# New durations in the cost model that orders a fused attention, FFN and soft-MoE kernel

## The chip, the cores and the metric

The kernel runs on one core of one Trainium2 chip. The metric is the device time of one execution in microseconds (us). The engines are PE (TensorE), DVE (VectorE), ACT (ScalarE), POOL (GpSimd) and SP (SyncE). Each works through its own list of instructions strictly in the order in which the program holds them; an instruction whose inputs are not there holds up everything behind it on its engine.

## The reference

Three stages follow each other, all in float32:

```python
# 1. thresholded attention: q, k, v are (4, 8, 576, 64)
scores = matmul(q, k.T) / 8
thresh = max(scores, -1) - tau
attn = softmax(where(scores >= thresh, scores, -1e9))
x = matmul(attn, v)                     # as (2304, 512)
# 2. FFN: w_in (512, 2048), w_out (2048, 512)
x = relu(x @ w_in)**2 @ w_out
# 3. soft MoE over 2304 tokens, 32 slots, 8 experts
logits = x @ phi
slot_input = softmax(logits, 0).T @ x
slot_out = relu(slot_input[e] @ w1[e]) @ w2[e]   # for each expert e
out = softmax(logits, 1) @ slot_out
```

The weights w_in and w_out reach the chip as 64-bit numbers and are turned into float32 there.

## The kernel before

**The parts of the work.** The conversion takes the two FFN weight matrices in 32 chunks of 128x512: a load on SP (L273), scaling on ACT (`c_scale`, L279), two bit steps on DVE (`c_low` L289, `c_shift` L293), the sign on POOL or DVE (`c_flip` L302, `c_sign` L304). A chunk of w_in is then split into a high and a low part (`c_hi` L319 on ACT, `c_lo` L320 on POOL). A chunk of w_out is turned on PE, multiplied with phi and stored to DRAM (`c_store`, L341).

Attention runs over 16 pairs of heads of five tiles each, 80 tiles in all; the last tile of a pair is mixed and half as large. One tile goes through a chain: the scores on PE (`s`, L477 and L482, or L471 and L474 for a mixed tile), and then for each of its two heads `top` on DVE (L498), `expo` on ACT (L510), `bound` on POOL (L504) and `keep` on DVE (L514). There is one PSUM buffer for the scores, so the scores of the next tile wait for both `top` of this one. From the second batch on, 36 tiles are turned by DMA: `high` on ACT (L532), `low` on POOL (L536), and a DMA transpose on SP (`dturn`, L543); two such tiles make a group, and the group ends with `av` on PE (`av_split`, L635 and L640), which needs both transposes. There are 18 such groups. The other tiles are turned on PE (L241). `hl` (the input of a transpose) has two buffers, `pt` (its output) two.

The FFN has nine units of 256 tokens. A unit is 16 halves of 12 matmuls (`f_a`, `f_b`, L932), followed by relu and square on ACT or DVE, and by a chain of smaller steps towards the slots (L747 to L870). The first half waits for all 32 converted chunks. When attention has ended, the expert weights are loaded, and after the last unit a tail that is written out by hand (`tail`, up to L1176) computes the experts and the output.

**What sets the order.** All of this except the tail is given to a list planner (`Plan`, L31 to L133). Each step has an engine, a modelled duration, a key, the steps it depends on and the buffers it takes and gives back. The planner simulates the engines: whenever one is free it starts, among the steps that are ready by the model and have their buffers, the one with the smallest key. FFN steps have keys on PE above all others (`FKEY`, 1e5), so PE takes them when no attention or conversion step is ready. The modelled durations therefore decide the order of the instructions and nothing else: a semaphore still guards each dependency on the chip. A step that follows another is ready 0.17 (`HOP`) after it. A DMA is modelled as `DMA_LEAD` 1.13, its time on a shared bus, and `DMA_TAIL` 0.95; a transpose also holds SP until its bus time less the tail:

```python
self.bus = max(self.bus, self.now + DMA_LEAD) + o.dma
o.end = max(self.bus, o.end + DMA_LEAD) + DMA_TAIL
if o.turn:
    self.free[o.eng] = max(self.now + o.cost, self.bus - DMA_TAIL)
```

Of the kernel before, what the change touches and what calls it, by code (L numbers as in the profile page):

```python
# [139 lines left out]
def tile_kernel(  # L140
# [26 lines left out]
    NU = 256  # L167
# [45 lines left out]
    def add(kind, eng, cost, fn, deps=(), key=0.0, *args, **kw):  # L213
        return plan.add(eng, cost, fn, deps, key + LEAD.get(kind, 0.0), *args, **kw)
# [41 lines left out]
    def conv_ops():  # L256
# [10 lines left out]
        def chunk(n, w, r0, c0):  # L267
# [72 lines left out]
            g = add("c_turn", "PE", 0.6, turn, [s], k, ["mm", "wt"])  # L340
# [3 lines left out]
            pr = add("c_prod", "PE", 1.05, prod, [e, lphi], k, rel=[("wt", g)])  # L344
# [8 lines left out]
    def attn_ops():  # L353
# [56 lines left out]
        def split_v(x):  # L410
# [39 lines left out]
            sc = add("v_scale", "DVE", 0.5, scales, [st], k0, rel=[("mm", st)])  # L450
# [4 lines left out]
        def tiles(p):  # L455
# [5 lines left out]
            def tile_ops(n, j):  # L461
# [23 lines left out]
                S_ = add("s", "PE", 1.4, s_mm, d["ready"], k, ["s"])  # L485
# [3 lines left out]
                for a in heads:  # L489
# [28 lines left out]
                    X = add("top", "DVE", 0.89, top, [S_], k, ["u"] + (["sm"] if first_g and not a else []), [("s", S_)])  # L518
                    if first_g and not a:
                        gd["first"] = X  # L520
                    h = add("bound", "POOL", 0.52, bound, [X], k)
                    E_ = add("expo", "ACT", 0.77, expo, [X] + ([ee] if a else []), k, [] if a else ["e"])
# [22 lines left out]
                if by_dma(p, g) and not mixed:  # L545
                    ls = []
                    for a in heads:
                        k = key(p, n * TA + a * TA / 2)
                        h = add("high", "ACT", 0.68, lambda a=a: high(a), [ks[a]] + ([hl] if a else []), k, [] if a else ["hl"])
                        hl = hl if a else h  # L550
                        ls.append(add("low", "POOL", 1.72, lambda a=a: low(a), [h], k, rel=[("e", ee)]))
                    k = key(p, n * TA + TA / 2)
                    t = add("dturn", "SP", 3.0, dturn, ls, k, [] if "pto" in gd else ["pt"], [("hl", hl)], dma=-6.8)
# [28 lines left out]
                for x in heads + (2,):  # L582
                    k = key(p, n * TA + min(x, 1) * TA / 2)
                    dep = ks if x == 2 else [ks[x]]
                    new = [] if "pto" in gd else [pk]
                    t = add("turn", "PE", 0.13 if x == 2 else 0.49, lambda x=x: turn(x), dep + [gd.get("pto")], k, ["mm"] + new, [(tag, ee)])
                    v_ = add("p_evac", "ACT", 0.27 if x == 2 else 0.59, lambda x=x: evac(x), [t], k, [], [("mm", t)])
                    gd.setdefault("pto", t)
                    gd.setdefault("turn", []).append(v_)

            def group_ops(g, n):
# [16 lines left out]
                rc = add("recip", "DVE", 0.5, recip, gd["keep"], k, ["rp"], [("sm", gd["first"])])  # L608
# [52 lines left out]
                if g < 2:  # L661
                    rc = add("spread", "POOL", 0.6, spread, [rc], k, ["rb"], [("rp", rc)])
# [13 lines left out]
                rt = add("r_turn", "PE", 0.13 if g == 2 else 0.26, rturn, [rc], k, ["mm", "rr"], rel)  # L676
                rc = add("r_evac", "ACT", 0.3 if g == 2 else 0.4, revac, [rt], k, [], [("mm", rt)])
                deps = gd["turn"] + [d["v_op"], d["vr_op"]]
                first = None
                if by_dma(p, g):  # L680
                    o = first = add("av", "PE", 1.9, av_split, deps + [d["vs_ready"]], k, ["ma"],
                                    [("pt", gd["pto"]), ("vh", d["vs_op"])])
                for lo, hi_ in () if by_dma(p, g) else ((0, 5),) if g == 2 else ((0, 2), (2, 5)):
                    c = (hi_ - lo) * (0.51 if g < 2 else 0.3) 
# [7 lines left out]
                ev = add("evac", "DVE", 0.25 if g == 2 else 0.45, evac, [o, rc], k, ["xp"] if g < 2 and kk == 0 else [], rel)  # L692
# [34 lines left out]
    def ffn_ops(units):  # L727
# [9 lines left out]
        def post(u, d, first, last):  # L737
# [77 lines left out]
            a0 = add("f_pl", "PE", 1.53, lambda: pl(0, MC // NG - 1), d["sq"][:-2], pk(), ["mm"])  # L815
            a = add("f_pm", "PE", 0.51, lambda: pl(MC // NG - 1, MC // NG), [a0] + d["sq"][-2:], pk())
            a2 = add("f_l4", "ACT", 0.26, lambda: nc.scalar.activation(l4, w["pl"][:, :NU], AF.Copy), [a], HI, ["l4"], [("mm", a0)])
            b_ = add("f_p12", "PE", 0.43, p12, [a2], pk(), ["mm"])
            bk = add("f_p1k", "PE", 0.35, p1k, [b_], pk(), [], [("l4", a2)])
            c = add("f_max", "DVE", 0.45, rowmax, [b_, fo.get("nm")], HI)  # L820
            e = add("f_alpha", "ACT", 0.5, alpha, [c, fo.get("nm")], HI, ["dT"], [("mm", b_)])
            f = add("f_total", "DVE", 0.12, total, [e, fo.get("ss")], HI)
            g = add("f_cmax", "DVE", 0.39, cmax, [bk], HI + 1)
            h = add("f_ce", "ACT", 0.15, lambda: nc.scalar.activation(w["ce"], w["ce"], AF.Exp), [g], HI + 1)
            add("f_csum", "DVE", 0.80, csum, [h], HI + 1, rel=[("mm", b_)])
            i_ = add("f_p3", "PE", 0.25, p3, [e], pk(), ["mm"], [("dT", e)])
            j_ = add("f_dk", "DVE", 0.2, dkc, [i_], HI, rel=[("mm", i_)])
            lastsg, turns = fo.get("sg"), []
            for t in range(T):
                gks, ro = [], []  # L830
                for j in range(NG):
# [23 lines left out]
                    ro.append(add("f_gk", "DVE" if dv else "ACT", 0.6 if dv else 0.49, evac, [tt], HI + 2, rel=[("mm", tt)]))  # L855
# [21 lines left out]
                for t_, (accum, merge, ro, gks) in enumerate(turns):  # L877
                    joint = last and t_
                    ac = add("f_acc", "PE", 0.93, accum, ro + [j_] + ([ac0] if joint else []), pk(), [] if joint else ["mm"], gks)
# [8 lines left out]
        for n, u in enumerate(units):  # L888
# [17 lines left out]
            for kk in range(KC):  # L906
# [3 lines left out]
                l = add("xlo", "DVE" if dv else "POOL", 0.35 if dv else 0.69, lambda f=xlo, kk=kk: f(kk), [h] + ls[:1],  # L910
# [5 lines left out]
            for m2 in range(MC // 2):  # L916
# [31 lines left out]
                a = add("f_a", "PE", 1.31, lambda f=mm_half: f(0), hs + ls + ms[-1:] + (conv if n == 0 else []), pk(), ["mm", "gt"])  # L948
                b_ = add("f_b", "PE", 1.31, lambda f=mm_half: f(1), [a], pk())
# [293 lines left out]
```

## Time and profile before

| what | value |
|---|---|
| three runs | 695.98, 696.82, 704.65 us; median 696.82 |
| span of the profiled execution | 694.8 us |
| PE busy | 630.1 us (91% of the span) |
| DVE busy | 456.8 us (66%) |
| ACT busy | 393.2 us (57%) |
| POOL busy | 233.1 us (34%) |
| DMA engines | 104.74 MB, 52% of 16 engines' span |
| mean granted PE clock | 0.979 |

The profile shows one execution. Its own time is not recorded apart from its span, from the first to the last instruction; the median of the three runs is 2.0 us above that span. Busy time counts an instruction until its result is written, so two that follow each other closely overlap a little. Where an engine waited, the row names what ended the wait.

### The profile page before, as it was taken

To read this page: it belongs to the slowest core of one execution; us is meant where nothing else is said; L and a number is where in the kernel's file an instruction comes from. 1 tells how busy PE (TensorE), PEld (TensorE's weight loads), DVE (VectorE), ACT (ScalarE), POOL (GpSimd) and SP (SyncE) were. 2 spreads that over 40 slices of the span, in tenths; PEclk is the share of its full clock that TensorE was granted. 3 is DMA by queue.
4 is the path that set the end of the run, shared out by engine and by line. 5 is a ranking of instruction groups with operands and counts; after the bars stand their busy time and mean duration, and the time that the engine had idled before them with its cause. 6 is when DMAs were issued, how large, how long until landed. Compare 5 with 4: busy or idle time off the path is not lost.

```text
span 694.8 us, 13413 instructions
## 1 busy us (share of the span) xinstructions
PE 630.1 (91%) x5084; PEld 458.4 (66%) x5084; DVE 456.8 (66%) x1183; ACT 393.2 (57%) x762; POOL 233.1 (34%) x308
## 2 busy tenths in 40 slices
PE   1566988999999999999999999999999999998883
PEld 0333656677857686677778667877788989883321
DVE  6999998975787868777966797778733132222503
ACT  4776756766765764766667557757653333331203
POOL 4866433212643434354244344344440000000000
PEclk9987999999999999999999999999999999999998
DMA  6854676422633545163437235352533940397987
GB/s 230 296 180 150 202 246 220 147 93 52 122 70 87 122 70 116 40 135 66 91 73 117 56 69 123 69 122 53 86 59 119 401 174 31 124 371 267 388 321 272
DMA packets 123056, 104.74 MB, mean 151 GB/s; under 512 B 90736, under 2 KB 95856, under 8 KB 122992
## 3 DMA queue, kind: packets, MB, share of 16 engines
q1 hardware_dynamic: 122992, 103.89, 52.0%
q8 instruction: 40, 0.66, 0.4%
q14 instruction: 24, 0.20, 0.1%
HBM read 73.73 MB, written 8.91 MB: 119 GB/s over the span
## 4 chain that ended last, share of the span: by engine, by line
PE 74%; DVE 10%; DMA 5%; ACT 4%; issue 4%; POOL 1%; SPq 0%; DVEq 0%; POOLq 0%; ACTq 0%
PE mm L932 30%; PE mm L241 11%; PE s L482 8%; PE po L627 4%; DVE e L514 3%; PE po L635 3%; PE mm L861 2%; PE mm L747 2%; PE mm L1063 2%; DMA w<-in_moe_w_dram 2%; PE s L477 2%; DMA w_out<-cv 2%; PE s L471 2%; DVE cv L293 2%; ACT e L510 1%
## 5 line engine op out<-in xcount | busy, mean ns | idle before, releaser
L932 PE MATMUL mm<-xh,w 128*128 128x256 f32 x1152 | 167.1, 288 | 0.0
L932 PEld LDWEIGHTS mm<-xh,w 128*128 128x128 f32 x1152 | 147.4, 191 | 16.7 <-issue 10.5
L514 DVE SCALAR_TENSOR_TENSOR e<-u,sm,e 128x576 f32<-128x576 f32 x144 | 125.4, 885 | 26.1 <-ACT e L510 22.9
L498 DVE TENSOR_SCALAR_CACHE_REDUCE u<-s,nscale 128x576 f32<-128x576 f32 x144 | 115.3, 811 | 26.0 <-PE s L482 20.5
L510 ACT ACTIVATE e<-u,sm 128x576 f32<-128x576 f32 x144 | 109.3, 775 | 38.7 <-DVE u L498 36.4
L536 POOL TENSOR_TENSOR hl<-e,hl 128x576 f16<-128x576 f32 x72 | 95.5, 1337 | 84.6 <-ACT hl L532 69.9
L504 POOL TENSOR_SCALAR sm<-sm,tau_p 128x1 f32<-128x1 f32 x144 | 60.7, 424 | 141.1 <-DVE u L498 108.9
L932 PE MATMUL mm<-xl,w 128*128 128x256 f32 x576 | 92.4, 283 | 0.0
L938 ACT ACTIVATE gt<-mm 128x512 f32<-128x512 f32 x72 | 42.9, 596 | 83.3 <-PE mm L932 82.8
L932 PEld LDWEIGHTS mm<-xl,w 128*128 128x128 f32 x576 | 79.3, 192 | 0.0
L482 PE MATMUL s<-kt,qt 64*128 64x512 f32 x256 | 77.0, 680 | 0.0
L241 PE MATMUL mm<-ident_r,e 128*128 128x128 f32 (+1 forms) x332 | 53.3, 296 | 6.0 <-DVE e L514 5.2
L241 PEld LDWEIGHTS mm<-ident_r,e 128*128 128x128 f32 (+1 forms) x332 | 39.9, 151 | 26.8 <-issue 10.0
L477 PE MATMUL s<-kt,qt 128*128 128x128 f32 x128 | 27.2, 295 | 31.0 <-DMA qt<-in_q_dram 11.8
L532 ACT ACTIVATE hl<-e 128x576 f16<-128x576 f32 x72 | 48.1, 679 | 11.8 <-DVE e L514 11.5
L579 ACT ACTIVATE pt<-mm 128x512 f32<-128x512 f32 x72 | 41.7, 594 | 21.9 <-PE mm L241 21.6
L944 DVE SCALAR_TENSOR_TENSOR gt<-mm,gt 128x512 f32<-128x512 f32 x18 | 12.4, 690 | 61.1 <-ACT gt L938 60.3
L477 PEld LDWEIGHTS s<-kt,qt 128*128 128x128 f32 x128 | 20.8, 199 | 36.1 <-issue 19.7
L627 PE MATMUL po<-pt,raw 128*64 128x64 f32 (+1 forms) x480 | 42.0, 309 | 0.0
L241 PE MATMUL mm<-ident_r,gt 128*128 128x128 f32 x288 | 38.3, 278 | 1.4 <-DVE ar L813 1.4
L241 PEld LDWEIGHTS mm<-ident_r,gt 128*128 128x128 f32 x288 | 31.5, 142 | 12.1 <-issue 8.2
L946 ACT ACTIVATE gt<-gt 128x512 f32<-128x512 f32 x54 | 33.9, 627 | 1.1
(148 smaller groups left out, 889.4 us busy)
## 6 DMA issues: line engine op xcount, KB each, us to landing
w<-in_moe_w_dram SPq DMA_DIRECT2D x25, 1024.0 KB, 11.9
raw<-in_moe_w_in_dram SPq DMA_DIRECT2D x16, 512.0 KB, 4.3
raw<-in_moe_w_out_dram SPq DMA_DIRECT2D x16, 512.0 KB, 4.0
kt<-in_k_dram SPq DMA_DIRECT2D x20, 320.0 KB, 3.3
qt<-in_q_dram SPq DMA_DIRECT2D x20, 320.0 KB, 3.7
raw<-in_v_dram SPq DMA_DIRECT2D x20, 256.0 KB, 3.1
w_out<-cv SPq DMA_DIRECT2D x16, 256.0 KB, 4.7
w<-w_out SPq DMA_DIRECT2D x4, 1024.0 KB, 9.1
```

The lines of the kernel that those rows point to most:

```text
L241: nc.tensor.transpose(out_, in_, ident[:n, :n])
L477: nc.tensor.matmul(s[:, 1].rearrange("p (c s) -> p c s", s=64)[:, 0:8:7], lt, d["kt"][:, 512:SQ], start=True, stop=True)
L482: nc.tensor.matmul(s[:, 2 * a], lt[i], d["kt"][i, 0:512], start=True, stop=True)
L498: nc.vector.tensor_scalar(u, o["s"][:, s0:s0 + S], nscale, None, ALU.mult, ALU.min, accum_out=gd["sm"][:, c:c + 1])
L504: nc.gpsimd.tensor_scalar(sm[:, 4 + c:5 + c], sm[:, c:c + 1], tau_p, None, ALU.add)
L510: nc.scalar.activation(e, o["u", a], AF.Exp, scale=-1.0, bias=gd["sm"][:, c:c + 1])
L514: nc.vector.scalar_tensor_tensor(e, o["u", a], sm[:, 4 + c:5 + c], e, ALU.is_le, ALU.mult, accum_out=sm[:, 8 + c:9 + c])
L532: nc.scalar.activation(o["hl"][:, a * S:(a + 1) * S], o["e"][:, a * S:(a + 1) * S], AF.Copy)
L536: nc.gpsimd.tensor_tensor(o["hl"][:, (2 + a) * S:(3 + a) * S], o["e"][:, c], o["hl"][:, c], ALU.subtract)
L627: nc.tensor.matmul(po[i, :n_], lt, rh, start=m == 0, stop=m == 4)
L932: nc.tensor.matmul(o["h"][:, i * NU:(i + 1) * NU], a, c, start=n_ == 0, stop=n_ == len(terms) - 1)
L938: nc.scalar.activation(g, o["h"], AF.Relu)
```

## The change

39 lines with modelled durations get new values; keys, buffers, dependencies and the instructions themselves stay. The core of the diff, with all that concerns attention and the FFN halves:

```diff
-            a = add("c_scale", "ACT", 0.53, scale, [l], k, ["cv"])
+            a = add("c_scale", "ACT", 0.57, scale, [l], k, ["cv"])
...
-                return add("c_lo", "POOL", 1.23, ...
+                return add("c_lo", "POOL", 1.4, ...
...
-                S_ = add("s", "PE", 1.4, s_mm, d["ready"], k, ["s"])
+                S_ = add("s", "PE", 1.28 if mixed else 1.38, s_mm, d["ready"], k, ["s"])
...
-                    X = add("top", "DVE", 0.89, top, ...
+                    X = add("top", "DVE", 0.75, top, ...
...
-                    h = add("bound", "POOL", 0.52, bound, [X], k)
-                    E_ = add("expo", "ACT", 0.77, expo, ...
+                    h = add("bound", "POOL", 0.26, bound, [X], k)
+                    E_ = add("expo", "ACT", 0.67, expo, ...
...
-                    K_ = add("keep", "DVE", 0.92, keep, [E_, h], k, rel=[("u", X)])
+                    K_ = add("keep", "DVE", 0.75, keep, [E_, h], k, rel=[("u", X)])
...
-                        h = add("high", "ACT", 0.68, ...
+                        h = add("high", "ACT", 0.58, ...
...
-                        ls.append(add("low", "POOL", 1.72, ...
+                        ls.append(add("low", "POOL", 1.28, ...
...
-                    t = add("dturn", "SP", 3.0, dturn, ls, k, ..., dma=-6.8)
+                    t = add("dturn", "SP", 2.75, dturn, ls, k, ..., dma=-3.2)
...
-                    o = first = add("av", "PE", 1.9, av_split, ...
+                    o = first = add("av", "PE", 1.83, av_split, ...
...
-                a = add("f_a", "PE", 1.31, ...
-                b_ = add("f_b", "PE", 1.31, ...
+                a = add("f_a", "PE", 1.44, ...
+                b_ = add("f_b", "PE", 1.44, ...
```

**What it moves: PE, the fourth of the 18 groups.** The first four rows are the mixed tile's `av`, and two transposes; then come the scores of a tile and FFN matmuls. Before:

```order
L627 MATMUL po<-pt,raw 64x64 x8
L627 MATMUL po<-pt,vbd_113 64x64 x2
L241 MATMUL mm<-ident_r,rb 128x128 x2
L241 MATMUL mm<-ident_r,rp 128x128
L477 MATMUL s<-kt,qt 128x2x64
L482 MATMUL s<-kt,qt 128x512 x2
L932 MATMUL mm<-xh,w_118 128x256
L932 MATMUL mm<-xh,w_119 128x256
```

Two halves of the FFN (24 matmuls) follow the scores there, then the scores of the next tile, two more halves, and only then the group's `av`. Now, at the same group:

```order
L477 MATMUL s<-kt,qt 128x2x64
L482 MATMUL s<-kt,qt 128x512 x2
L241 MATMUL mm<-ident_r,rb 128x128 x2
L747 MATMUL mm<-gt,wphi 32x256 x16
L241 MATMUL mm<-ident_r,e 128x128 x4
L241 MATMUL mm<-ident_r,e 64x128
L241 MATMUL mm<-ident_r,gt 128x128 x4
L241 MATMUL mm<-ident_r,rp 128x128
L477 MATMUL s<-kt,qt 128x2x64
L482 MATMUL s<-kt,qt 128x512 x2
L635 LDWEIGHTS vh
L635 MATMUL po<-pt,vh 64x256
```

The `av` now stands right behind the scores of the third tile after its group, where four tiles with more FFN work between them stood before.

**SP, the first transposes.** Loads of the next pair (`kt`, `qt`, `raw`) and DMA transposes share this queue. Before:

```order
L543 DMA_TRANSPOSE pt<-hl 128x18x128
L401 DMA kt<-in_k_dram 128x640
L543 DMA_TRANSPOSE pt<-hl 128x18x128
L401 DMA qt<-in_q_dram 128x640
L396 DMA raw<-in_v_dram 128x2x256
L543 DMA_TRANSPOSE pt<-hl 128x18x128 x3
```

Now:

```order
L543 DMA_TRANSPOSE pt<-hl 128x18x128 x2
L401 DMA kt<-in_k_dram 128x640
L401 DMA qt<-in_q_dram 128x640
L396 DMA raw<-in_v_dram 128x2x256
L543 DMA_TRANSPOSE pt<-hl 128x18x128 x3
L401 DMA kt<-in_k_dram 128x640
```

The two loads that stood between and behind the first two transposes now stand behind both.

**DVE, the first attention tile.** Conversion chunks (L289, L293, L304) and attention steps (L498, L514) share DVE at the start. Before:

```order
L293 SCALAR_TENSOR_TENSOR cv<-cv,raw_130 128x512
L304 SCALAR_TENSOR_TENSOR cv<-raw_130,cv 128x512
L289 TENSOR_SCALAR raw_148<-raw_148 128x512
L498 TENSOR_SCALAR u,sm<-s,nscale 128x576
L293 SCALAR_TENSOR_TENSOR cv<-cv,raw_148 128x512
L289 TENSOR_SCALAR raw_156<-raw_156 128x512
L498 TENSOR_SCALAR u,sm<-s,nscale 128x576
L293 SCALAR_TENSOR_TENSOR cv<-cv,raw_156 128x512
L289 TENSOR_SCALAR raw_176<-raw_176 128x512
L304 SCALAR_TENSOR_TENSOR cv<-raw_156,cv 128x512
L293 SCALAR_TENSOR_TENSOR cv<-cv,raw_176 128x512
```

Now:

```order
L293 SCALAR_TENSOR_TENSOR cv<-cv,raw_130 128x512
L304 SCALAR_TENSOR_TENSOR cv<-raw_130,cv 128x512
L498 TENSOR_SCALAR u,sm<-s,nscale 128x576 x2
L289 TENSOR_SCALAR raw_159<-raw_159 128x512
L514 SCALAR_TENSOR_TENSOR e,sm<-u,sm,e 128x576
L293 SCALAR_TENSOR_TENSOR cv<-cv,raw_159 128x512
L289 TENSOR_SCALAR raw_161<-raw_161 128x512
L514 SCALAR_TENSOR_TENSOR e,sm<-u,sm,e 128x576
L293 SCALAR_TENSOR_TENSOR cv<-cv,raw_161 128x512
L289 TENSOR_SCALAR raw_176<-raw_176 128x512
L304 SCALAR_TENSOR_TENSOR cv<-raw_161,cv 128x512
```

The two `top` of the first tile stood two conversion steps apart, the second one six rows below the last step of the fourth chunk; they now follow each other, ahead of the fifth chunk.

## Rows read from the trace of the kernel before

**Rows 1.** Busy time by stage; columns: stretch, length, each engine, granted PE clock, DMA share, GB/s.

```profile
0.00:17.00 17.00, 2.78 (x6) 1.01 (x6) 11.29 (x20) 6.91 (x11) 7.74 (x12) 1.00 0.69 235
17.00:70.00 53.00, 33.56 (x138) 18.35 (x138) 51.62 (x95) 37.71 (x67) 39.18 (x37) 0.86 0.62 208
70.00:122.00 52.00, 46.85 (x329) 32.67 (x330) 46.58 (x118) 35.05 (x68) 20.27 (x25) 0.95 0.70 222
122.00:156.00 34.00, 33.58 (x281) 24.38 (x278) 27.98 (x84) 24.54 (x52) 7.37 (x15) 1.00 0.36 117
156.00:520.00 364.00, 358.35 (x3042) 270.87 (x3042) 269.39 (x738) 237.34 (x468) 153.71 (x213) 1.00 0.43 85
520.00:618.00 98.00, 96.98 (x849) 86.72 (x850) 25.44 (x67) 35.34 (x67) 2.90 (x4) 1.00 0.51 191
618.00:695.00 77.00, 57.96 (x452) 24.37 (x451) 24.51 (x66) 16.33 (x33) 1.90 (x2) 0.94 0.84 317
```

**Rows 2.** Waits of PE, 0 to 156 us: total us, times, longest.

```profile
PE s L477 <- DMA qt<-in_q_dram: 11.8, 1, 11.8
...
PE s L477 <- DVE u L498: 6.6, 1, 6.6
```

**Rows 3.** The chain of waits, 98 to 106 us: start us, us, what.

```profile
99.28 5.93 DMA w_out<-cv
```

**Rows 4.** Groups of instructions, 156 to 520 us: busy us, mean ns, idle before.

```profile
L536 POOL TENSOR_TENSOR hl<-e,hl 128x576 f16<-128x576 f32 x72 | 95.5, 1337 | 84.6 <-ACT hl L532 69.9 <-issue 14.1 <-POOL xl L903 0.2
L514 DVE SCALAR_TENSOR_TENSOR e<-u,sm,e 128x576 f32<-128x576 f32 x106 | 89.1, 856 | 22.1 <-ACT e L510 19.4 <-POOL sm L504 2.2 <-issue 0.4
```

**Rows 5.** The same view, 0 to 156 us.

```profile
L514 DVE SCALAR_TENSOR_TENSOR e<-u,sm,e 128x576 f32<-128x576 f32 x38 | 36.4, 967 | 4.0 <-ACT e L510 3.6 <-ACT cv L279 0.2 <-POOL sm L504 0.2
```

**Rows 6.** Timeline of PE, ACT, SP: the first, seventh, third group; start us, us.

```profile
167.01 1.13 PE L482 MATMUL s<-kt,qt 64*128 64x512 f32 x4
...
176.23 2.67 SPq L543 DMA_TRANSPOSE pt<-hl  x1
...
188.81 1.50 PE L635 MATMUL po<-pt,vh 128*64 128x256 f16 x24
...
287.98 1.13 PE L482 MATMUL s<-kt,qt 64*128 64x512 f32 x4
...
300.57 2.74 SPq L543 DMA_TRANSPOSE pt<-hl  x1
...
190.90 1.13 PE L482 MATMUL s<-kt,qt 64*128 64x512 f32 x4
...
206.29 1.24 ACT L532 ACTIVATE hl<-e 128x576 f16<-128x576 f32 x2
...
210.58 2.67 SPq L543 DMA_TRANSPOSE pt<-hl  x1
```

**Rows 7.** Landing of the transposes, line 543, all 36.

```profile
DMA to landing us min/median/max: 4.5/4.6/6.3
```

**Rows 8.** Pieces of PE work in the chain of waits: start us, us, what.

```profile
155.95 1.44 PE mm L932 x12
159.48 1.06 PE s L482 x4
...
135.39 1.88 PE po L627 x16
...
198.56 1.05 PE s L471 x2
...
213.74 1.46 PE mm L241 x12
...
552.45 2.04 PE mm L747 x32
```

**Rows 9.** The chain of waits in the tail.

```profile
656.10 13.41 DMA w<-in_moe_w_dram
```

More of the change, by code (lines that the diff above doesn't have):

```diff
@@ L308, in chunk @@
             l = add("c_load", "SP", 0.5, load, key=k - 8, acq=["raw64"], dma=1.46)
-            a = add("c_scale", "ACT", 0.53, scale, [l], k, ["cv"])
-            t = add("c_low", on, 0.53 if on == "ACT" else 0.35, low, [l], k)
+            a = add("c_scale", "ACT", 0.57, scale, [l], k, ["cv"])
+            t = add("c_low", on, 0.57 if on == "ACT" else 0.34, low, [l], k)
             s = add("c_shift", "DVE", 0.61, shift, [a, t], k)
             if flip:
-                s = [s, add("c_unit", "ACT", 0.53, unit, [a], k)]
-                s = add("c_flip", "POOL", 1.25, sign, s, k, rel=[("raw64", l)])
+                s = [s, add("c_unit", "ACT", 0.57, unit, [a], k)]
+                s = add("c_flip", "POOL", 1.31, sign, s, k, rel=[("raw64", l)])
             else:
@@ L516, in keep @@
                         )
-                    X = add("top", "DVE", 0.89, top, [S_], k, ["u"] + (["sm"] if first_g and not a else []), [("s", S_)])
+                    X = add("top", "DVE", 0.75, top, [S_], k, ["u"] + (["sm"] if first_g and not a else []), [("s", S_)])
                     if first_g and not a:
                         gd["first"] = X
-                    h = add("bound", "POOL", 0.52, bound, [X], k)
-                    E_ = add("expo", "ACT", 0.77, expo, [X] + ([ee] if a else []), k, [] if a else ["e"])
+                    h = add("bound", "POOL", 0.26, bound, [X], k)
+                    E_ = add("expo", "ACT", 0.67, expo, [X] + ([ee] if a else []), k, [] if a else ["e"])
                     if not a:
                         ee = E_
-                    K_ = add("keep", "DVE", 0.92, keep, [E_, h], k, rel=[("u", X)])
+                    K_ = add("keep", "DVE", 0.75, keep, [E_, h], k, rel=[("u", X)])
                     gd.setdefault("keep", []).append(K_)
@@ L548, in tile_ops @@
                         k = key(p, n * TA + a * TA / 2)
-                        h = add("high", "ACT", 0.68, lambda a=a: high(a), [ks[a]] + ([hl] if a else []), k, [] if a else ["hl"])
+                        h = add("high", "ACT", 0.58, lambda a=a: high(a), [ks[a]] + ([hl] if a else []), k, [] if a else ["hl"])
                         hl = hl if a else h
-                        ls.append(add("low", "POOL", 1.72, lambda a=a: low(a), [h], k, rel=[("e", ee)]))
+                        ls.append(add("low", "POOL", 1.28, lambda a=a: low(a), [h], k, rel=[("e", ee)]))
                     k = key(p, n * TA + TA / 2)
-                    t = add("dturn", "SP", 3.0, dturn, ls, k, [] if "pto" in gd else ["pt"], [("hl", hl)], dma=-6.8)
+                    t = add("dturn", "SP", 2.75, dturn, ls, k, [] if "pto" in gd else ["pt"], [("hl", hl)], dma=-3.2)
                     gd.setdefault("pto", t)
@@ L606, in spread @@
                     nc.gpsimd.tensor_copy(gd["rb"].rearrange("p (t a d) -> p t a d", t=2, a=2), y)
-                rc = add("recip", "DVE", 0.5, recip, gd["keep"], k, ["rp"], [("sm", gd["first"])])
+                rc = add("recip", "DVE", 0.32, recip, gd["keep"], k, ["rp"], [("sm", gd["first"])])
                 def av(lo, hi):
@@ L661, in group_ops @@
                 if g < 2:
[L662 removed]
+                    rc = add("spread", "POOL", 0.38, spread, [rc], k, ["rb"], [("rp", rc)])
                 def rturn():
@@ L691, in group_ops @@
                 rel = [("ma", first), ("rr", rt)] + ([("mx", d["vs_op"])] if by_dma(p, g) else [])
-                ev = add("evac", "DVE", 0.25 if g == 2 else 0.45, evac, [o, rc], k, ["xp"] if g < 2 and kk == 0 else [], rel)
+                ev = add("evac", "DVE", 0.42 if g == 2 else 0.4, evac, [o, rc], k, ["xp"] if g < 2 and kk == 0 else [], rel)
                 ev_at.setdefault("rem" if g == 2 else (b, g), []).append(ev)
@@ L854, in post @@
                     dv = j in GKD
-                    ro.append(add("f_gk", "DVE" if dv else "ACT", 0.6 if dv else 0.49, evac, [tt], HI + 2, rel=[("mm", tt)]))
+                    ro.append(add("f_gk", "DVE" if dv else "ACT", 0.6 if dv else 0.48, evac, [tt], HI + 2, rel=[("mm", tt)]))
                 def accum(t=t):
@@ L909, in ffn_ops @@
                 dv = kk in SPH
-                l = add("xlo", "DVE" if dv else "POOL", 0.35 if dv else 0.69, lambda f=xlo, kk=kk: f(kk), [h] + ls[:1],
+                l = add("xlo", "DVE" if dv else "POOL", 0.34 if dv else 0.71, lambda f=xlo, kk=kk: f(kk), [h] + ls[:1],
                         HI, [] if kk else ["xl"], [] if u == "rem" else [("xp", xdeps[0])])
```

44 lines of the change are left out of this document (22 added, 22 removed).

## Prediction

> **What bounds the kernel now.** I read the engines' busy time by stage first [rows 1]. PE's idle time in the seven stages is 14.2, 19.4, 5.2, 0.4, 5.7, 1.0 and 19.0 us, 64.9 of the 695.0 in all. So there are three regimes. Up to 122 us the conversion of the weights holds PE back: DVE is busy 51.6 of 53.0 us between 17 and 70. From 122 to 618 us PE works 488.9 of 496 us, and the other engines have room (DVE 269.4 of 364.0 while attention and FFN run together). The last 77 us are the hand-written tail. Since all PE work is in the program before and after, the time moves only by what is added to or taken from these 64.9 us: the question is where PE will wait.
>
> In the front PE's longest waits are for the first load, 11.8 us, and for the second `top` of the first tile, 6.6 us [rows 2]; later the chain of waits goes through a store of converted weights, 5.9 us [rows 3]. In the middle I looked at the steps of attention: `keep` takes 856 ns in the mean and `low` 1337 [rows 4]; in the front `keep` takes 967 [rows 5]. Last I followed groups that are turned by DMA, from the end of the scores of their second tile to the issue of the second transpose and to `av` [rows 6], with the time that a transpose needs to land [rows 7].
>
> **The change, part by part.**
>
> *The order.* The planner's DVE and ACT steps become 13 to 18% shorter, `low` 26%; a transpose holds SP for 3.38 instead of 6.98 in the model (1.13 + 3.2 - 0.95 against 1.13 + 6.8 - 0.95). A half of the FFN becomes longer, 1.44 instead of 1.31; the chain of waits has 1.44 for 12 such matmuls [rows 8], so that number is right. The result on PE: before, 55 of the 144 FFN halves stand behind the scores of the last tile, now 76. At 1.44 us, 30 us of FFN work move from between the tiles to behind them. This is no saving: PE does the same work, and where it does nothing but FFN work (520 to 618 us) it is idle 1.0 us [rows 1].
>
> *The front.* The first four chunks and the order of their loads stay. The two `top` of the first tile now follow each other, so the second scores need not wait 6.6 us. But DVE is full there: what attention gains, the conversion loses, and FFN work can start only when all 32 chunks are done. Counted over DVE's list, four more `top` and one more reciprocal pair stand ahead of the last step of the conversion, 4 x 0.86 (the price of `keep`, [rows 4]) and 0.3 (the diff's new value), 3.7 us; PE has one more tile's scores ahead of its first FFN matmul, 1.06 us [rows 8] and two small matmuls. Between 122 and 156 us PE is busy 33.6 of 34.0 us, so the work done earlier there is work not done later. I put the front at 0. If DVE sets the start of the FFN instead, it costs 3.7 us; if the new order of stores and loads removes what PE idles between 70 and 122 us, it gains 5.2.
>
> *The middle, the cover of the transposes.* In the first group 20.7 us passed between the end of the scores (167.01 + 1.13) and `av` (188.81), while the transpose was issued 8.1 us after the scores and landed 4.6 us later, 12.7 us in all [rows 6, 7]. So `av` had 8 us to spare. In the new order I counted the PE work between the same two places, with prices from [rows 8]. In the fourth group: 11 transposes 1.34, two FFN halves 2.88, an `av` of the other kind 1.88 and 0.24, mixed scores 1.05 and 0.24, two scores 2 x 1.30, L747 2.04, 12 transposes 1.46: together 13.7 us. The 18 groups have, in order, 14.0, 15.8, 18.9, 13.7, 14.8, 15.8, 15.1, 23.4, 18.1, 15.9, 17.1, 18.9, 24.1, 55.8, 56.2, 49.0, 19.7 and 18.1 us; before, none had under 19. If all need the 12.7 us of the first, nothing waits: 0. If they need what the seventh needed, 11.5 us to the issue (289.11 to 300.57) and 4.6 to land, 16.1, then seven are short, by 2.1, 0.3, 2.4, 1.3, 0.3, 1.0 and 0.2 us, together 7.6. I take 2: nearer to the lower end, since both the new order of ACT and POOL and the shorter hold of SP work for the short case. On the other side, the most that a better order can take from the stretch 156 to 520 us is its idle 5.7 us; I count none of it.
>
> What queues behind a late `av`: everything on PE, the next scores first, and with them DVE, whose next `top` reads those scores. A stall there is paid in full.
>
> *The port that DVE and POOL share.* Between 0 and 156 us `keep` takes 967 ns against 856 later [rows 4, 5]; the plan now gives it 0.75. The longer means stand beside more POOL work, 74.6 of 156 us against 153.7 of 364.
>
> The Trainium skill ("SBUF — State Buffer", section "Who interferes with whom") says why: a DVE instruction with two SBUF inputs and a GpSimd instruction that reads SBUF exclude each other, and the second one blocks until the first ends. `keep` and `low` are such a pair, and denser attention speaks against the change by that rule. If each group's last `keep` waited out one whole `low` (1.3 us), 12.7 would become 14.0 and the sum would grow by 0.3 us, at the fourth group; the means of the trace show far less than a whole `low` for each.
>
> *The tail.* Its instructions and SP's last rows from the expert weights on are the same. Its longest piece is a load, 13.4 us from 656.1 us on [rows 9]; those loads take the place of tiles that the last FFN unit frees, so they move with the end of the FFN. Cost 0.
>
> *Sum.* 0 + 2 + 0 = +2 us on the span of 694.8. What lies around the span is 2.0 us (the median of the runs, 696.8, less the span), so the forecast is **699 us**, no change that a measurement of this kernel can tell: the bound is 2%, 13.9 us, that is 682.9 and 710.8.
>
> **The rivals.**
>
> *A better order all over (faster).* The new durations of PE, `av` and `low` are nearer to the rows. If PE's waits between 156 and 520 us vanish (5.7) and the idle time between 70 and 122 us with them (5.2), the time is 696.8 - 10.9 = 686. For it: those idle times exist. Against it: the old order already keeps PE at 98.4% there, because its durations for all engines but PE were too long and left cover.
>
> *The cover is gone (slower).* The place is `av` behind the second transpose. Its price starts when scores to landing takes more than 13.7 us, and decides the result above about 17: at 18.0 us eight of the 18 groups are short by 4.0, 2.2, 4.3, 3.2, 2.2, 2.9, 2.1 and 0.9, together 22 us, 697 + 22 = 719. For it: the third group took 18.6 us to the issue alone (192.03 to 210.58). Against it: there `high` was issued only at 206.29 in a line of other work, as the planner had it wait for `hl` buffers that a long modelled transpose kept; that reason falls away.
>
> *The change does nothing.* Excluded: PE's, DVE's, ACT's and POOL's lists all differ, in over a thousand lines on PE.
>
> **Chances and range.** No change around 699 (692 to 706): 0.62. Better all over, 680 to 691: 0.22. Cover gone, 706 to 720: 0.16. Of the second about a quarter lies below 682.9, of the third somewhat over half above 710.8: faster by over 2% 0.05, within 2% 0.86, slower by over 2% 0.09. The range, with 0.1 left out on either side, is 685 to 710.
>
> **What would show each step.** In the new profile, PE's idle time up to its first L932 should be about 39 us, and that matmul start between 152 and 160 us. `av` (L635) should follow the landing of its second transpose by 0 to 6 us instead of 8; PE's waits in front of L635 should sum to 2 us, at most 8. The stretch with attention should end some 30 us earlier, and a longer stretch of nothing but FFN should follow, PE above 98% there, and the tail should take 77 us. The forecast is wrong if PE is idle over 15 us between its first L932 and the end of the FFN, or if the first L932 moves by more than 6 us.

## The result and the profile after

| | before | changed |
|---|---|---|
| median of 20 runs each, us | 698.99 | 707.91 |
| lowest and highest, us | 695.82, 704.65 | 703.75, 711.16 |
| span of the profiled execution, us | 694.8 | 706.7 |
| mean granted PE clock in it, as recorded | 0.979 | 0.969 |

The ratio is 1.0122, with a 95% interval of 1.010 to 1.0143. The changed kernel is slower by 8.9 us in the medians: within the 2% that the forecast called no change, inside its range, and 9 us above its 699.

Busy time by stage of the changed kernel, columns as in [rows 1]:

```profile
0.00:17.00 17.00, 2.77 (x6) 1.00 (x6) 11.24 (x19) 7.47 (x11) 8.97 (x13) 1.00 0.88 277
17.00:70.00 53.00, 33.24 (x139) 18.70 (x141) 52.25 (x96) 34.95 (x66) 36.90 (x36) 0.77 0.57 192
70.00:122.00 52.00, 50.26 (x359) 35.05 (x355) 46.64 (x120) 36.84 (x71) 18.16 (x26) 0.94 0.71 235
122.00:156.00 34.00, 31.36 (x223) 22.33 (x223) 24.36 (x72) 21.83 (x46) 9.32 (x16) 0.95 0.31 100
156.00:520.00 364.00, 350.99 (x2978) 263.87 (x2978) 267.95 (x741) 234.36 (x463) 153.12 (x210) 1.00 0.51 116
520.00:618.00 98.00, 96.96 (x839) 85.82 (x838) 27.22 (x71) 36.05 (x69) 4.37 (x6) 1.00 0.10 34
618.00:707.00 89.00, 68.39 (x551) 35.91 (x549) 25.19 (x67) 20.61 (x40) 1.90 (x2) 0.97 0.86 322
```

PE's idle time rose from 5.7 to 13.0 us in the stretch 156 to 520. The granted clock between 17 and 70 us reads 0.86 before and 0.77 now, but these two do not compare, as the paragraph on the clock below shows. Since attention ends earlier now, stages cut at each kernel's own landmarks compare better: up to the first L932, to the last scores, to the end of the FFN, the tail. The changed kernel:

```profile
0.00:157.90 157.90, 119.53 (x751) 78.68 (x751) 136.31 (x313) 103.00 (x196) 73.35 (x90) 0.89 0.59 193
157.90:474.20 316.30, 303.70 (x2529) 222.17 (x2528) 250.95 (x691) 213.40 (x423) 145.50 (x202) 0.99 0.48 96
474.20:630.50 156.30, 154.85 (x1368) 138.20 (x1370) 43.09 (x115) 59.57 (x114) 12.56 (x15) 1.00 0.36 127
630.50:706.70 76.20, 55.89 (x448) 23.63 (x440) 24.50 (x66) 16.16 (x33) 1.33 (x2) 0.96 0.84 316
```

The kernel before, cut in the same way:

```profile
0.00:155.70 155.70, 116.47 (x745) 76.11 (x746) 137.18 (x313) 103.91 (x195) 74.57 (x89) 0.93 0.60 196
155.70:502.40 346.70, 341.05 (x2877) 256.64 (x2876) 262.82 (x720) 228.94 (x451) 146.30 (x205) 1.00 0.44 87
502.40:618.70 116.30, 115.28 (x1026) 101.73 (x1028) 32.29 (x87) 44.26 (x85) 10.93 (x13) 1.00 0.48 171
618.70:694.80 76.10, 57.26 (x448) 23.89 (x440) 24.51 (x66) 16.11 (x33) 1.29 (x2) 0.94 0.84 316
```

The idle times of PE are 38.4, 12.6, 1.45 and 20.3 us against 39.2, 5.65, 1.0 and 18.8: 72.7 against 64.7 in all, 8.0 us more. PE's busy time for the same work is 634.0 against 630.1 us. The span is 11.9 us longer, and these two are all of it.

**Part of the added busy time is a lower clock.** I took every 5 us of a trace and multiplied PE's busy time there by one minus the granted clock; the sum is the busy time that the lower of the two levels (1.2 instead of 2.4 GHz) added. It is 9.4 us before and 14.5 after. But the records of the clock begin only at 34.2 us in the trace of before and at 21.6 in that of the changed kernel, and up to there the profile states 1.00 for want of a record. The same four matmuls of the scores, in the trace of before, ahead of its first record and behind it:

```profile
30.65 2.08 PE L482 MATMUL s<-kt,qt 64*128 64x512 f32 x4
38.10 1.13 PE L482 MATMUL s<-kt,qt 64*128 64x512 f32 x4
```

All such groups of four ahead of the first record take 2.08 us, in both traces, as does the one at 47.03 us of before, in a stretch recorded at the lower level: PE is at that level there. That adds half of PE's busy time in this stretch (12.2 and 6.4 us), 6.1 us before and 3.2 after. The whole loss to the clock is then 15.5 and 17.7 us, and busy time less this loss is 614.6 and 616.3. So the 11.9 us are 8.0 of waiting, 2.2 of clock and 1.7 that neither accounts for. As far as one profiled execution of each can tell, most of the 8.9 us in the medians is therefore waiting. The same gap in the records lies behind the 0.86 and 0.77 above: with the unrecorded part at the lower level they become 0.70 and 0.73.

**Which waits.** PE's waits between the first L932 and the last scores (total us, times, longest), changed:

```profile
PE mm L241 <- POOL rb L606: 2.5, 2, 1.4
PE mm L241 <- ACT pt L579: 1.4, 1, 1.4
PE mm L747 <- DVE gt L944: 1.1, 1, 1.1
PE s L477 <- DVE u L498: 1.1, 2, 0.8
...
PE po L635 <- DVE u L498: 0.9, 1, 0.9
PE po L635 <- DVE xr L648: 0.9, 1, 0.9
```

The list has fourteen entries, on DVE (4.7 us), ACT (4.3), POOL (2.5) and PE's own queue (0.8). Before, the whole list was four:

```profile
PE mm L861 <- DVE dk L810: 1.8, 2, 1.6
PE s L477 <- DVE u L498: 1.7, 1, 1.7
PE mm L241 <- DVE ar L813: 1.4, 2, 0.7
PE mm L241 <- DVE e L514: 0.7, 1, 0.7
```

No single wait took the place of another; there are many short ones, and ACT and POOL, on which PE never waited here before, now account for over half. One thing that grew is a queue on POOL. The groups of the three steps between 156 and 520 us:

```profile
L514 DVE SCALAR_TENSOR_TENSOR e<-u,sm,e 128x576 f32<-128x576 f32 x107 | 90.5, 859 | 21.9 <-POOL sm L504 12.1 <-ACT e L510 9.0
L536 POOL TENSOR_TENSOR hl<-e,hl 128x576 f16<-128x576 f32 x72 | 94.4, 1328 | 59.2 <-ACT hl L532 55.4 <-issue 2.0 <-POOL sm L504 1.3
L504 POOL TENSOR_SCALAR sm<-sm,tau_p 128x1 f32<-128x1 f32 x104 | 41.8, 406 | 100.1 <-DVE u L498 67.4 <-DVE sm L599 27.2 <-DMA pt<-hl 3.4
```

In [rows 4] DVE waited 2.2 us in front of `keep` for `bound` (`sm`, L504) and 19.4 for `expo`; now it is 12.1 and 9.0. `keep` itself takes 859 ns, as before (856). The new model gives `bound` 0.26, where this row has 406 ns (389 before). `keep` (0.75 in the model, 859 ns in its row) and `low` (1.28 and 1328) are shorter than the trace, too; the old values 0.52, 0.92 and 1.72 stood above it (389, 856 and 1337 before). The chain of waits of the changed kernel shows one such case:

```profile
236.83 0.69 ACT hl L532
237.52 0.07 issue
237.60 2.07 POOL hl L536 x2
239.67 0.44 issue
240.11 0.30 POOL sm L504
240.41 0.02 issue
240.43 0.04 DVE e L514
```

`bound` stands behind two `low` on POOL, which wait for `high`, and `keep` waits for `bound`. The whole piece of the chain off PE runs from 230.56 to 247.03; the pieces of the chain off PE, from the first L932 until attention is done, sum to 83 us, before to 39.

That this queue makes PE wait is not shown. DVE's whole idle time in front of `keep` is no longer than before, 21.9 against 22.1 us, and in the table below e2 has 3.0 us of it on `bound` and still 13.3 us of idle time on PE.

### The profile page after: what moved, and what is told of

Its sections match the earlier page's. It is cut to its first block, busy times and chain, and to the rows that moved or that the text cites. A ratio compares the mean times of both kernels' runs of the same rounds, so it can differ in the third digit from the quotient of the medians.

```text
span 706.7 us, 13443 instructions
## 1 busy us (share of the span) xinstructions
PE 634.0 (90%) x5084; PEld 462.7 (65%) x5084; DVE 454.8 (64%) x1183; ACT 392.1 (55%) x762; POOL 232.7 (33%) x308
## 4 chain that ended last, share of the span: by engine, by line
PE 67%; DVE 13%; DMA 6%; ACT 6%; issue 4%; POOL 1%; SPq 1%; DVEq 0%; ACTq 0%
PE mm L932 28%; PE mm L241 9%; PE s L482 7%; PE po L627 4%; DVE e L514 3%; PE po L635 3%; DVE u L498 3%; PE mm L861 2%; DMA w_out<-cv 2%; PE mm L747 2%; PE mm L1063 2%; DMA w<-in_moe_w_dram 2%; PE s L471 2%; PE s L477 2%; ACT e L510 1%
## 5 line engine op out<-in xcount | busy, mean ns | idle before, releaser
L932 PE MATMUL mm<-xh,w 128*128 128x256 f32 x1152 | 167.0, 287 | 0.4 <-ACT pt L579 0.4
L932 PEld LDWEIGHTS mm<-xh,w 128*128 128x128 f32 x1152 | 147.5, 191 | 17.3 <-issue 14.3
L514 DVE SCALAR_TENSOR_TENSOR e<-u,sm,e 128x576 f32<-128x576 f32 x144 | 125.5, 883 | 29.1 <-ACT e L510 15.6
L498 DVE TENSOR_SCALAR_CACHE_REDUCE u<-s,nscale 128x576 f32<-128x576 f32 x144 | 114.6, 809 | 21.3 <-PE s L482 19.8
L536 POOL TENSOR_TENSOR hl<-e,hl 128x576 f16<-128x576 f32 x72 | 94.4, 1328 | 59.2 <-ACT hl L532 55.4
L504 POOL TENSOR_SCALAR sm<-sm,tau_p 128x1 f32<-128x1 f32 x144 | 58.8, 412 | 133.2 <-DVE u L498 92.8
L932 PE MATMUL mm<-xl,w 128*128 128x256 f32 x576 | 92.4, 283 | 0.0
L932 PEld LDWEIGHTS mm<-xl,w 128*128 128x128 f32 x576 | 79.4, 192 | 0.0
L532 ACT ACTIVATE hl<-e 128x576 f16<-128x576 f32 x72 | 48.1, 682 | 11.9 <-DVE e L514 10.0
L627 PE MATMUL po<-pt,raw 128*64 128x64 f32 (+1 forms) x480 | 44.2, 319 | 0.2 <-ACT pt L579 0.2
L903 POOL TENSOR_TENSOR xl<-xp,xh 128x256 fp32r<-128x256 f32 x16 | 12.1, 768 | 95.3 <-PE mm L932 93.5
## 6 DMA issues: line engine op xcount, KB each, us to landing
w<-in_moe_w_dram SPq DMA_DIRECT2D x25, 1024.0 KB, 11.9
```

The source lines that it names most:

```text
L498: nc.vector.tensor_scalar(u, o["s"][:, s0:s0 + S], nscale, None, ALU.mult, ALU.min, accum_out=gd["sm"][:, c:c + 1])
L504: nc.gpsimd.tensor_scalar(sm[:, 4 + c:5 + c], sm[:, c:c + 1], tau_p, None, ALU.add)
L514: nc.vector.scalar_tensor_tensor(e, o["u", a], sm[:, 4 + c:5 + c], e, ALU.is_le, ALU.mult, accum_out=sm[:, 8 + c:9 + c])
L532: nc.scalar.activation(o["hl"][:, a * S:(a + 1) * S], o["e"][:, a * S:(a + 1) * S], AF.Copy)
L536: nc.gpsimd.tensor_tensor(o["hl"][:, (2 + a) * S:(3 + a) * S], o["e"][:, c], o["hl"][:, c], ALU.subtract)
L627: nc.tensor.matmul(po[i, :n_], lt, rh, start=m == 0, stop=m == 4)
```

## The experiments

They ran in three batches of four; in each the kernel before ran beside them on the same chip (medians 698.5, 699.9 and 699.7 us). Idle times are span less PE's busy time. "Low clock" is the sum over the recorded clock defined above, "start" half of PE's busy time ahead of the first record. The halves are the FFN halves (L932, 12 matmuls) behind the last scores, counted in the trace. The last column is DVE's idle time in front of `keep` put down to `bound`, 156 to 500 us.

| kernel | new on DVE, ACT, POOL | us | ratio (95%) | PE idle | of it first L932 to last scores | low clock | start | halves | `keep` on `bound` |
|---|---|---|---|---|---|---|---|---|---|
| before | no | 699.0 | 1 | 64.7 | 5.6 | 9.4 | 6.1 | 55 | 2.2 |
| e5_vector_back | no | 699.3 | 1.0009 (0.9985-1.0033) | 64.3 | 8.3 | 11.8 | 7.1 | 62 | 3.7 |
| e8_jitter_before2 | no | 704.3 | 1.0084 (1.006-1.0108) | 69.0 | 8.9 | 12.5 | 3.3 | 62 | 0.2 |
| e4_jitter_before | no | 704.7 | 1.0089 (1.0054-1.0125) | 66.3 | 6.6 | 17.4 | 5.7 | 58 | 1.2 |
| e1_pe_only | no | 705.5 | 1.0103 (1.0068-1.0138) | 68.1 | 10.6 | 14.4 | 5.9 | 59 | 1.6 |
| e12_more_slack | no | 706.1 | 1.0079 (1.0051-1.0106) | 64.2 | 6.7 | 16.1 | 8.8 | 60 | 1.9 |
| e3_transpose_only | no | 710.1 | 1.0152 (1.0108-1.0197) | 69.4 | 10.8 | 17.6 | 7.1 | 68 | 3.4 |
| e9_slack | x 1.15 | 709.3 | 1.0116 (1.0086-1.0145) | 65.6 | 10.8 | 18.3 | 6.3 | 75 | 7.7 |
| e11_actpool_back | DVE | 710.1 | 1.0128 (1.0092-1.0165) | 71.9 | 9.6 | 11.6 | 7.6 | 74 | 1.7 |
| e10_dve_back | ACT, POOL | 714.6 | 1.0195 (1.0165-1.0225) | 69.5 | 13.4 | 18.9 | 5.8 | 77 | 15.8 |
| changed | all | 707.9 | 1.0122 (1.010-1.0143) | 72.7 | 12.6 | 14.5 | 3.2 | 76 | 12.1 |
| e7_transpose_back | all | 714.3 | 1.0221 (1.0193-1.0248) | 76.9 | 16.4 | 11.5 | 3.0 | 72 | 6.3 |
| e2_vector_only | all | 718.1 | 1.0278 (1.023-1.0326) | 74.3 | 13.3 | 17.7 | 8.1 | 72 | 3.0 |
| e6_jitter_after | all | 719.1 | 1.0306 (1.0276-1.0336) | 75.9 | 18.5 | 16.2 | 8.3 | 76 | 8.1 |

**First batch: the change in parts, and a meaningless change.** e1 takes the new values of PE alone (14 lines, two shown):

```diff
-                S_ = add("s", "PE", 1.4, s_mm, d["ready"], k, ["s"])
+                S_ = add("s", "PE", 1.28 if mixed else 1.38, s_mm, d["ready"], k, ["s"])
-                a = add("f_a", "PE", 1.31, ...
+                a = add("f_a", "PE", 1.44, ...
```

> The kernel before with only the 14 lines of PE durations changed (f_a and f_b 1.44, the small PE steps). On PE 59 FFN halves stand behind the last tile (before 55, the change 76). Theory 'packing' (attention steps planned with short vector and transpose durations stand so densely that PE meets the ends of the lists of DVE and ACT): no change, 696 to 701 us, PE's idle time between its first L932 and the end of the FFN at most 8 us. Rival 'any new order' (the keys fit the old order and every reshuffle costs as much): 703 to 709 us. Rival 'the PE durations did it': 704 to 709 us.

e2 takes those of DVE, ACT and POOL alone:

```diff
-                    X = add("top", "DVE", 0.89, top, ...
+                    X = add("top", "DVE", 0.75, top, ...
-                        ls.append(add("low", "POOL", 1.72, ...
+                        ls.append(add("low", "POOL", 1.28, ...
```

> The kernel before with only the DVE, ACT and POOL durations changed; PE and the transposes keep the old ones. 72 FFN halves stand behind the last tile. Theory 'packing': slower than before, 702 to 707 us, with PE waiting for DVE and ACT between 156 and 520 us as in the change. Rival 'any new order': 703 to 709 us, so this run does not part the two. Rival 'the transposes did it' (the shorter hold of SP alone): 696 to 701 us.

e3 changes one line:

```diff
-                    t = add("dturn", "SP", 3.0, dturn, ls, k, ..., dma=-6.8)
+                    t = add("dturn", "SP", 2.75, dturn, ls, k, ..., dma=-3.2)
```

> The kernel before with only the line of the DMA transpose changed (2.75 and -3.2). The cover of av counted on PE shrinks as in the change (13 to 21 us), and 68 FFN halves stand behind the last tile. Theory 'packing': slower, 701 to 706 us, with no wait at av itself, since av in the change started 5.5 us or more after the issue of its transpose. Rival 'the vector durations did it': 696 to 701 us. Rival 'any new order': 703 to 709 us.

e4 keeps the old values and multiplies each kind's by a number between 0.98 and 1.02 drawn from its name:

```diff
+        cost *= 0.98 + 0.04 * (zlib.crc32((kind + 'a').encode()) % 1000) / 1000
         return plan.add(eng, cost, fn, deps, key + LEAD.get(kind, 0.0), *args, **kw)
```

> The kernel before with each kind's old duration multiplied by a factor between 0.98 and 1.02 that means nothing; it moves as many instructions as the change does. 58 FFN halves stand behind the last tile. Theory 'packing': no change, 695 to 702 us, since covers and density stay. Rival 'any new order': 703 to 709 us.

Measured: 705.5, 718.1, 710.1 and 704.7. The theory "packing" missed all four times: e1 and e4 came out 4.5 and 2.7 us above its ranges, with 11.9 us of idle time in e1 where at most 8 were allowed, and e3 and e2 4.1 and 11.1 us above. Even the meaningless change costs 6 us, in the profiled executions mostly clock (idle +1.6, low clock +8.0). The rival "any new order" held for e1 and e4, and e1 fits the rival that the PE values did it as well; e3 lies just above "any new order", e2 9 us above. The parts add up to 38 us and together cost 9: the times of single orders do not add.

**Second batch: the other way round.** e5 is the changed kernel with the old values on DVE, ACT and POOL (the lines of e2 undone).

> The changed durations of PE and SP (the transposes too) stay, those of DVE, ACT and POOL go back to the old, longer ones. Theory "no slack": the old DVE, ACT and POOL durations contain what a step costs beside its bare run time (the gap between two instructions, waiting for another engine), so an order made with them keeps PE fed: PE idle between its first L932 and the end of the scores at most 8 us (before 5.65, changed kernel 12.6), 699 to 705 us. Rival "any new order costs the same" (each reshuffle lowers the granted clock in some places, whatever the numbers): 703 to 709, the idle time without a rule.

e6 is the changed kernel with the factor of e4 (the same line).

> The changed kernel with every kind's duration multiplied by a meaningless factor between 0.98 and 1.02. Theory "no slack": the durations are still bare run times, so PE still idles 10 to 15 us between its first L932 and the end of the scores; 704 to 714 us. Rival "any new order": one draw of the same lot as the other reshuffles, 703 to 709, with an idle time anywhere between 5 and 14.

e7 is the changed kernel with the old transposes (the line of e3 undone).

> The changed durations of all engines, but the transposes' old ones (3.0 and 6.8). Theory "no slack": the short DVE, ACT and POOL durations remain, av has more cover but the small waits of PE stay: idle 10 to 15 us between the first L932 and the end of the scores, 706 to 714 us. Were the transposes' cover the cause, this kernel would go back to 697 to 702. Rival "any new order": 703 to 709.

e8 is e4 with `'b'` for `'a'` in its line.

> The old durations, each kind multiplied by another meaningless factor between 0.98 and 1.02. Theory "no slack": PE idle between its first L932 and the end of the scores stays at 5 to 8 us as in the first such kernel (6.6), time 697 to 705, what is lost is granted clock. Rival "any new order": 703 to 709, idle time anywhere between 5 and 14.

Measured: 699.3, 719.1, 714.3 and 704.3, idle times 8.3, 18.5, 16.4 and 8.9 us: "no slack" gave the side of each, though the sizes were off: the idle times lie 0.3, 3.5, 1.4 and 0.9 us above its bounds, e6's time 5 us and e7's 0.3. e8 fits the rival "any new order" in full. The rows of the middle (first L932 to last scores) of e5, then of e6:

```profile
148.20:492.90 344.70, 336.38 (x2844) 250.70 (x2845) 268.48 (x736) 228.62 (x456) 151.74 (x211) 1.00 0.45 90
```

```profile
160.40:484.70 324.30, 305.79 (x2520) 222.38 (x2518) 250.62 (x681) 212.43 (x418) 145.94 (x201) 0.98 0.47 93
```

With the new values of PE and the transposes but the old of the three other engines the time is that of before, so these two together cost nothing, and taking back the values of DVE, ACT and POOL takes back the changed kernel's whole loss. A loss of this size does not need them, though: the PE values alone cost 7.0 us (e1), the transposes alone 11.6 (e3). What goes with the short values is the long idle time. The meaningless factors moved the changed kernel by 11 us.

**Third batch: where the slack is needed.** e9 stretches the new values of eight attention steps:

```diff
+        cost *= 1.15 if kind in ("top", "keep", "recip", "bound", "low", "spread", "expo", "high") else 1.0
         return plan.add(eng, cost, fn, deps, key + LEAD.get(kind, 0.0), *args, **kw)
```

> The changed kernel with the new durations of the eight attention steps on DVE, ACT and POOL (top, keep, recip, bound, low, spread, expo, high) multiplied by 1.15; the conversion, the FFN, PE and the transposes keep the new values. Theory "no slack": what the bare run times lacked is slack, and any slack will do, not the old numbers: PE idle between its first L932 and the end of the scores at most 9 us (changed kernel 12.6), 699 to 705 us. Rival "other steps or chance": it stays with the kernels that have new DVE, ACT and POOL durations, 706 to 719, idle 12 to 18.

e10 is the changed kernel with DVE's old values:

```diff
-                    K_ = add("keep", "DVE", 0.75, keep, ...
+                    K_ = add("keep", "DVE", 0.92, keep, ...
```

> The changed kernel with the old durations on DVE alone (top, keep, recip and the small ones of the FFN). Theory "no slack", in the form that DVE is where it counts, since most waits of PE in the slower kernels are put down to DVE: 699 to 705 us, idle at most 9 us between the first L932 and the end of the scores. Rival "the slack is needed on ACT and POOL" (the chain expo, high, low behind each keep): it stays at 706 to 714, idle 10 to 16.

e11 is the changed kernel with the old values of ACT and POOL:

```diff
-                    h = add("bound", "POOL", 0.26, bound, [X], k)
+                    h = add("bound", "POOL", 0.52, bound, [X], k)
```

> The changed kernel with the old durations on ACT and POOL alone. Theory "no slack", in the form that DVE is where it counts: DVE's short top, keep and recip still let PE's next scores stand too early, 706 to 714 us, idle 10 to 16 us between the first L932 and the end of the scores. Rival "the slack is needed on ACT and POOL": 699 to 705, idle at most 9.

e12 is e5 with the line of e9 and 1.1 for 1.15.

> New durations of PE and of the transposes, old ones on DVE, ACT and POOL (the kernel that came out like the one before, 699.3), and the eight attention steps on those engines longer by a further 10%. Theory "no slack": there is enough slack already; more takes little of the 8.3 us of idle time that are left between the first L932 and the end of the scores (5 to 8 us), 696 to 702 us. Rival "any new order": 703 to 709.

Measured: 709.3, 714.6, 710.1 and 706.1. Here the theory missed. e9 did not come back to 699 to 705: PE's idle time fell by 7.1 us in all, but the clock cost 24.6 us with the start, 6.9 more than in the changed kernel. DVE is not where it counts: e10 came out at 714.6, just above the range of the rival "the slack is needed on ACT and POOL", and with DVE's old values the waits stay. The group of `keep`, 156 to 500 us, in e10 and then in e11:

```profile
L514 DVE SCALAR_TENSOR_TENSOR e<-u,sm,e 128x576 f32<-128x576 f32 x106 | 89.0, 852 | 30.3 <-POOL sm L504 15.8 <-ACT e L510 14.2
```

```profile
L514 DVE SCALAR_TENSOR_TENSOR e<-u,sm,e 128x576 f32<-128x576 f32 x106 | 91.9, 886 | 7.2 <-ACT e L510 5.3 <-POOL sm L504 1.7
```

The old values of ACT and POOL take the wait on `bound` from 12.1 to 1.7 us and PE's idle time in the middle from 12.6 to 9.6, but e11's time does not follow: its first L932 comes at 162.5 us and its front idles 41.7. So e11 fits neither: its time is in the range of "DVE is where it counts", its idle time of 9.6 lies between the two. e12 shows from the other side that idle time is not all: 64.2 us idle, like before, and 706, the time of "any new order", through a lower clock (24.9 us with the start, against 15.5).

**What the fourteen orders show together.** The six with old values on the three engines (before left out) idle 64.2 to 69.4 us, the four with all new ones 72.7 to 76.9: the means are 66.9 and 75.0, 8.1 us apart. Their losses to the clock, with the start, are nearly the same, 21.3 and 20.6 us in the means. So the values of DVE, ACT and POOL set the waiting, and the clock differs from order to order, 14.5 to 25.8 us, without going with the values; before has one of the lowest, 15.5. In time the six average 705.0 us and the four 714.9: against before, an order made with the old values on these engines also costs some 6 us, and the changed kernel is the fastest of the four with all new ones. The idle time in the middle also goes with the halves left behind the last scores (correlation 0.78): 5.6 to 10.6 us with 55 to 62 of them, 9.6 to 18.5 with 68 to 77. That fits a reason (less FFN work stands between the tiles to fill PE while DVE, ACT and POOL finish a step), but no run holds the halves fixed and changes only the packing, so it is argued, not shown. None of the orders beats the kernel before.

## Why the prediction was right, and where it was not

**The order.** 21 more halves behind the last tile were forecast; the trace has 76 against 55. The last scores start 28.2 us earlier (474.2 against 502.4; some 30 forecast), and PE is at 99.1% in the stretch of FFN work alone (over 98%). "No saving" was right. That it costs nothing was the step that failed: PE idles 7.0 us more while attention runs. That the moved halves had filled PE there fits the orders above, and is argued, not shown.

**The front.** Forecast 0, between +3.7 and -5.2. PE idles 38.4 us up to the first L932 (39 forecast), which starts at 157.9 (152 to 160 forecast). The idle time after 70 us did go down from 5.15 to 1.7 us, and 2.6 came up between 122 us and the first L932.

**The cover of the transposes.** Forecast +2, from 0 to 7.6; measured 0. In the first group (timeline, start and length; then the group of its two transposes, and their landing):

```profile
162.46 1.13 PE L482 MATMUL s<-kt,qt 64*128 64x512 f32 x4
...
178.40 1.50 PE L635 MATMUL po<-pt,vh 128*64 128x256 f16 x24
```

```profile
L543 SPq DMA_TRANSPOSE pt<-hl x2: 2694/2806/2917, 167.0 to 171.0; - x2
DMA to landing us min/median/max: 4.6/4.6/4.7
```

From the scores to `av` pass 178.40 - 163.59 = 14.8 us; 14.0 had been counted from the order. The second transpose is issued at 171.0, 7.4 us after the scores, and lands at 175.6, 2.8 us ahead of `av`. In 15 of the 18 groups the issue comes 7.1 to 11.8 us after the scores, and in none does `av` wait for a landing; the two waits in front of L635, 1.8 us, are DVE's. It was close: the second transpose of the sixth group lands 0.1 us ahead of `av`, that of the last 0.5, where the least was 4.7 before; so 0 instead of 2 is in part luck. The shorter hold of SP did what the prediction said; the rival "the cover is gone" did not occur, and its 719 in e2 and e6 has another cause: in front of L635 PE waits for a landing not at all in e2, and for 0.7 us in e6.

**The rest of the middle.** Forecast 0, "the most that a better order can take is 5.7". That bounded only a gain. A loss had the same right: the prediction itself said that the old durations of all engines but PE "left cover", used this against the faster rival, and did not price what goes when that cover goes. It measured 7.0 us. In all, PE idles 14.1 us between its first L932 and the end of the FFN, just under the 15 at which the forecast was to count as wrong.

**The port.** `keep` was looked at for the cost of denser attention. It takes 859 ns in the mean in the middle (856 before) and 949 in the front (967): no more than before. The Trainium skill ("SBUF — State Buffer", section "Who interferes with whom") has the second of such a pair block for the whole of the first. Single rows of the trace agree: of two `keep` in a row the second, which started beside a `low`, took 1.83 us instead of 0.81.

```profile
331.89 0.81 DVE L514 SCALAR_TENSOR_TENSOR e<-u,sm,e 128x576 f32<-128x576 f32 x1
332.00 3.61 POOL L536 TENSOR_TENSOR hl<-e,hl 128x576 f16<-128x576 f32 x2 [0.66 <-ACT hl L532]
332.63 1.83 DVE L514 SCALAR_TENSOR_TENSOR e<-u,sm,e 128x576 f32<-128x576 f32 x1
```

A small step that was not looked at, of `recip` on L599, did take longer. Its rows between 156 and 520 us, before and now:

```profile
L599 DVE TENSOR_SCALAR sm<-sm 128x4 f32<-128x4 f32 (+1 forms) x36 | 11.5, 319 | 0.3
L599 DVE TENSOR_SCALAR sm<-sm 128x4 f32<-128x4 f32 (+1 forms) x36 | 16.7, 463 | 0.2
```

Its longest, 1.1 us where the median is 0.16, end within 0.03 us of the `low` that ran beside them. These are 5.2 us more of DVE; e2 has 203 ns in this row and PE idles as long, so they are not shown to be PE's loss. POOL also slowed DVE through the order of its own list (`bound` behind `low`).

**The tail.** Forecast 77 us, measured 76.2 (76.1 before). Its long load is the same as in [rows 9]:

```profile
672.96 13.53 DMA w<-in_moe_w_dram
```

**The sum.** +2 forecast, +8.9 in the medians. The base moved, too: the median of before is 699.0 in 20 runs, 696.8 in the three that the forecast had. Two terms were missing: 7.0 us of short waits, and the clock (2.2 us between the profiled executions). The class was right because both are small beside 2%, not because the place of the loss was seen: 707.9 lies in the band 706 to 720 that the forecast gave to "the cover is gone", with a chance of 0.16, and that rival's mechanism did not occur. Single orders of one kind differ by 11 us (699.3 to 710.1, 707.9 to 719.1). Idle time and the clock with the start make up nearly all of that: 5.1 and 5.8 us between e5 and e3, 3.2 and 6.8 between the changed kernel and e6. Why an order gets the one clock or the other remains open.

## What to carry to other kernels

In a list planner a modelled duration also decides how much filler is left between the steps. Set shorter than the steps' own rows in the trace, as here on DVE, ACT and POOL, the durations packed the critical work and pushed the filler behind it, and PE waited more. When a change shifts an order, price the loss of cover as well as the gain, for every engine whose figures shrink. And before an order is credited or blamed, run a few orders from meaningless changes of the same table: here they moved the time by 4, 6 and 11 us.

## What the runs showed of the hardware

The granted clock is worth more here than expected. In all fourteen traces PE works at the lower level until the records of the clock begin, at 21 to 43 us (2.08 us for four matmuls of the scores instead of 1.13). PE falls to its lower level in the middle of the kernel, too, after short idle times, though not after each. The changed kernel without a fall, and at the restart of attention after a pause, in steps of 5 us:

```profile
230.00:235.00 5.00, 2.85 (x21) 2.06 (x21) 4.56 (x18) 2.78 (x6) 3.64 (x6) 1.00 0.90 184
235.00:240.00 5.00, 5.00 (x37) 3.40 (x37) 4.61 (x12) 3.11 (x6) 2.74 (x3) 1.00 0.57 104
...
450.00:455.00 5.00, 3.86 (x33) 2.12 (x33) 3.40 (x8) 4.97 (x11) 1.21 (x2) 1.00 0.00 0
455.00:460.00 5.00, 3.93 (x27) 2.38 (x21) 4.93 (x14) 3.27 (x6) 2.66 (x4) 1.00 0.16 31
460.00:465.00 5.00, 4.66 (x33) 2.79 (x33) 4.38 (x11) 4.40 (x10) 3.43 (x4) 0.70 0.62 115
```

And e1:

```profile
270.00:275.00 5.00, 3.13 (x34) 2.05 (x34) 4.97 (x12) 2.34 (x6) 3.10 (x3) 1.00 0.24 45
275.00:280.00 5.00, 4.60 (x19) 2.99 (x19) 3.55 (x16) 2.09 (x4) 0.31 (x1) 0.60 0.90 208
```

PE idled 1.1 us in either of two stretches, or 1.9 in one, all at full clock, and the granted clock was 0.70 or 0.60 just behind; at 230 us it idled 2.1, and nothing fell. So a wait can be paid twice, once as idle time and once as slower work, and which wait is could not be told from these rows. One and the same order also gets different clocks: over 50 executions of the kernel before, time and mean granted clock, as far as recorded, go together (correlation -0.80), from 704.8 us at 0.960 to 697.6 at 0.984.
